# V projected in four 32-column tiles at once, three rounds for four pieces

## The chip, the cores and the metric

The kernel runs on one NeuronCore of a Trainium2 chip. The core has a matrix engine (TensorE, PE in the profile; its weight loads are PEld), a vector engine (VectorE, DVE), a scalar engine (ScalarE, ACT), GpSimd (POOL) and SyncE (SP), which here issues the DMAs that bring weights in. PSUM, where TensorE writes, is handed out in eight tiles by four pools. The metric is device microseconds for one execution.

## What is computed

Four blocks follow each other: A, B, A, B, each added to its input after a layernorm (the same weights both times). A is an attention with a recurrent memory: the 2048 tokens go in 64 segments of 32, and each segment attends over 8 memory rows and its own 32 tokens, with 32 heads of 192. The memory rows of one segment's output are the memory of the next, so segments can't be computed at once. B is a local attention over 8 keys at a distance of 2, with 32 heads of 20.

```python
for s in range(n_seg):
    h = jnp.concatenate([mem, x[:, s*32:(s+1)*32, :]], axis=1)
    q = jnp.einsum('btd,dhe->bhte', h, Wq)
    k = jnp.einsum('btd,dhe->bhte', h, Wk)
    v = jnp.einsum('btd,dhe->bhte', h, Wv)
    scores = jnp.where(mask, jnp.einsum('bhqe,bhke->bhqk', q, k) * scale, -1e9)
    o = jnp.einsum('bhqk,bhke->bhqe', _softmax(scores), v)
    o = jnp.einsum('bhte,hed->btd', o, Wo)
    mem = o[:, :8, :]
    outs.append(o[:, 8:, :])
...
x = x + A(layernorm(x)); x = x + B(layernorm(x))
x = x + A(layernorm(x)); x = x + B(layernorm(x))
```

D is 640 (five chunks of 128 rows, `NCH`), and q, k and v have 6144 columns each.

## The kernel before

**Steps and lanes.** `run` (L517) makes 66 steps and one last. In a step the first A block works on segment s and the second A block on segment s - 2 (`LAG`), side by side as two lanes, so that each weight that is loaded serves 2 x 40 rows: 8 memory rows and 32 tokens for each lane. The rows lie transposed in `ST` (L181), 128 rows of D by chunk, lane and position; there are two such tiles, one for this step and one for the next. Each lane has 64 positions (`SLOT`), of which 40 are used and the rest are zero. The B blocks of the two lanes are done in the same step with the output of the step before.

**Weights.** The four A matrices are cut into 64 halves of 480 KB (`half`, L218): 32 for q and k, 16 for V, 16 for the output. 26 of them stay in SBUF after the first step (`RESIDENT`); the other 38 are read again in every step, from copies in DRAM (`Wr`) that POOL's queue wrote in the first step, into a ring of 7 buffers (`wt`), issued on SP's queue in the order in which they are used. A call of `half` returns a resident tile if there is one; for another half it takes a ring buffer and issues its transfer.

**Order.** The order of TensorE's work is written out by hand in `stages` (L51), and the same in each step; the other engines' instructions are ordered by a scheduler as their inputs come. The names in the plan are:
- q: `qk` (L296), 30 matmuls with 80 moving columns; ACT copies the result to `QK` (L306).
- s: `scores` (L308), 32 small matmuls for a group of four head pieces, then the softmax: three DVE operations, an exp on ACT, three more on DVE, the last of which writes `Pm` (L334).
- t: `p_transpose` (L337), four transposes, and two copies to `PT`, the upper half on DVE and the lower on ACT. PT holds zeros where a lane's queries would meet the other lane's keys.
- v: `v` (L346). The stationary operand is one chunk of `ST` with both lanes, 2 x 64 positions = 128 columns, and the moving one 384 columns of a V half; five matmuls add up a piece in `v_ps`. ACT copies even pieces and DVE odd ones to `vt` (L356, L358). There are 16 pieces, four to a group.
- pv: `pv` (L361), the product of probabilities and V for two pieces, 12 matmuls in two tiles of 64 columns; ACT copies it to `ot`.
- o: `o` (L374), 15 matmuls with `Wo` that add to `acc`; acc holds one of three PSUM tiles of the pool `psA` from the first o to the end of the step; q and v take turns in the others.
- ln1, qkv, logits, e, wo, ln2, store: the B blocks. ln1 and ln2 (`ln_stats`, L271) need a square on POOL (L274) and a sum on DVE (`ssq`, L276) before their last matmul (L280). logits (L444) uses four tiles of 32 columns. e (`b_expand`) has four matmuls and two DVE operations of 0.68 and 1.02 us, five times a step.

At the end of a step `finish_step` writes the memory rows of the next step's `ST` from acc (L395) on DVE; q0 of the next step waits for them.

Of the kernel before, what the change touches and what calls it, by code (L numbers as in the profile page):

```python
# [19 lines left out]
P = 128  # L20
# [9 lines left out]
NP_ = 16  # L30
# [20 lines left out]
def stages():  # L51

    plan = [("q", 0), ("q", 1), ("alpha", 0), ("q", 2), ("q", 3), ("ln1", 0)]
    plan += [("q", 4), ("s", 0), ("v", 0), ("q", 5), ("v", 1), ("qkv", 0), ("q", 6), ("t", 0), ("v", 2), ("q", 7), ("v", 3)]
    for g in (2, 3):
        i, j = 4 * g, 2 * (g - 2)
        extra = [[], [], [("logits", 0)], [("input", 0)], []] if g == 2 else [[("e", c)] for c in range(5)]
        plan += [("q", i), ("s", g - 1)] + extra[0] + [("pv", j), ("v", i - 4)] + extra[1] + [("pv", j + 1), ("q", i + 1)] + extra[2]
        plan += [("o", 2 * j), ("o", 2 * j + 1)] + extra[3] + [("v", i - 3), ("q", i + 2), ("t", g - 1), ("v", i - 2)] + extra[4]
        plan += [("o", 2 * j + 2), ("o", 2 * j + 3), ("q", i + 3), ("v", i - 1)]  # L60
    plan += [("s", 3), ("pv", 4), ("v", 12), ("pv", 5), ("o", 8), ("o", 9), ("v", 13), ("wo", 0), ("v", 14), ("v", 15), ("t", 3)]
    plan += [("o", 10), ("ln2", 0), ("pv", 6), ("pv", 7), ("o", 11), ("store", 0)]
    return plan + [("o", k) for k in range(12, 16)]
# [5 lines left out]
def consumption_order():  # L69

    order = []
    for what, i in PLAN:
        if what == "q":
            order += [2 * i, 2 * i + 1]
        elif what in "vo":
            order.append((32 if what == "v" else 48) + i)
    return order


ORDER = consumption_order()  # L80
RESIDENT = {ORDER[(2 * i + 1) * N_HALVES // (2 * N_RESIDENT)] for i in range(N_RESIDENT)}

# [25 lines left out]
class Kernel:  # L108
    def __init__(self, ctx, tc, A_x, A_mem0, A_Wq, A_Wk, A_Wv, A_Wo, B_wqkv, B_wo, out):
# [16 lines left out]
        self.vp = pool("vp", 6)  # L126
# [6 lines left out]
    def constants(self):  # L133
# [12 lines left out]
        for u in range(2):  # L146
# [3 lines left out]
            nc.gpsimd.memset(m1[SLOT * u:SLOT * u + NM, :], 0.0)  # L150
        self.maskA = cp.tile([P, LT], BF16, name="maskA")
# [34 lines left out]
        self.Pm = [cp.tile([P, 4, 2, SLOT], BF16, name=f"Pm{i}") for i in range(2)]  # L186
# [3 lines left out]
        for t in self.PT:  # L190
            nc.gpsimd.memset(t[:], 0.0)
# [104 lines left out]
    def qk(self, i):  # L296
# [3 lines left out]
        for k in range(2):  # L300
            w = self.half(2 * i + k)[:, :].rearrange("p (c n) -> p c n", c=NCH)
            for m in range(3):
                for c in range(NCH):
                    nc.tensor.matmul(ps[:, 3 * k + m, :, :], lhsT=w[:, c, m * P:(m + 1) * P], rhs=st[:, c, :, 0:LT],  # L304
                                     start=(c == 0), stop=(c == NCH - 1))
# [40 lines left out]
    def v(self, i):  # L346
        nc = self.nc
        w = self.half(32 + i)[:, :].rearrange("p (c n) -> p c n", c=NCH)
        st = self.ST[self.step % 2]
        ps = self.psA.tile([P, UW], F32, name="v_ps", tag="A")  # L350
        for c in range(NCH):
            nc.tensor.matmul(ps[:, :], lhsT=st[:, c, :, :].rearrange("p l t -> p (l t)"), rhs=w[:, c, :],  # L352
# [256 lines left out]
```

## Time and profile before

| what | value |
|---|---|
| median of 3 runs | 3828.19 us (3825.26 to 3828.8) |
| profiled execution, device time | 3827.25 us |
| its span (first to last instruction) | 3825.5 us |
| mean granted TensorE clock | 0.982 |
| read from HBM in all | 1251.42 MB |
| DMA in the first 95 us, by share of 16 engines | 1.04, 353 GB/s |
| end of the first step (first ST from acc, L395) | 149.7 us |
| end of the last full step (last ST from acc) | 3796.5 us |
| mean of the 65 steps between | 56.1 us |
| V matmuls (L352), 128 x 384 | 5280, 330 ns each from start to modelled end, busy 1050 us |
| q and k matmuls (L304) | 31680, busy 1480 us |
| matmuls of logits (L444), four 32-column tiles | 1320, busy 31.9 us |

A matmul's 330 ns is the time from its start to the end of its last row; matmuls overlap, and five V matmuls that stand together occupy TensorE for 0.82 us, as the order of time shows. "Busy" is the time in which at least one was under way. PE's idle time is what other engines, or transfers, or instruction supply ("issue": nothing that the profile shows was waited for) cost it.

### The profile page before, as it was taken

The numbers are of one execution on the slowest core, as the hardware profiler recorded it, in microseconds if no ns is written. First come the engines' busy times: TensorE is split into PE (matmuls) and PEld (weight loads), VectorE is DVE, ScalarE is ACT, GpSimd is POOL, SyncE is SP. The second block draws the span as 40 slices with busy tenths as digits, with TensorE's granted clock in tenths as the row PEclk, the third lists the DMA queues.
The fourth block names the chain that finished last, engine by engine and source line by source line (L and its number), as shares of the span: only waits on it lengthen the run. The fifth ranks groups of instructions, "written<-read, shape, count | busy, mean of one in ns | idle before, by whom it ended". The sixth has DMA issues, their size and how long they took to land.

```text
span 3825.5 us, 172799 instructions
## 1 busy us (share of the span) xinstructions
PE 3515.1 (92%) x79035; PEld 2998.4 (78%) x79035; DVE 2042.5 (53%) x4660; ACT 1501.6 (39%) x3213; POOL 372.0 (10%) x475
## 2 busy tenths in 40 slices
PE   5799999999999999999999999999999999999997
PEld 3578788787888878788787887887788788788886
DVE  1355555545555555555555555555555555555554
ACT  1243443444344344344334434443443444344443
POOL 3110010001001001000100100110010010011000
PEclk7799999999999999999999999999999999999998
DMA  9999999999999999999999999999999999999995
GB/s 353 376 331 341 340 334 344 330 328 337 343 341 337 339 338 338 322 344 341 327 339 340 339 339 342 343 336 331 334 335 338 342 336 346 320 342 342 337 347 211
DMA packets 403276, 1283.94 MB, mean 336 GB/s; under 512 B 41704, under 2 KB 83312, under 8 KB 402544
## 3 DMA queue, kind: packets, MB, share of 16 engines
q1 hardware_dynamic: 397200, 1251.58, 91.4%
q0 software_dynamic: 3040, 18.68, 1.2%
q8 instruction: 617, 10.11, 1.1%
q10 hardware_dynamic: 2304, 2.62, 0.2%
q14 instruction: 115, 0.94, 0.1%
HBM read 1251.42 MB, written 21.30 MB: 333 GB/s over the span
## 4 chain that ended last, share of the span: by engine, by line
PE 74%; DVE 15%; DMA 5%; issue 3%; ACT 1%; SPq 1%; POOLq 0%; POOL 0%; ACTq 0%
PE qk_ps L304 26%; PE v_ps L352 20%; PE acc L385 12%; DVE oT L475 5%; DVE prodv L473 4%; PE qkv_ps L428 4%; PE o_ps L368 3%; PE s_ps L322 3%; PE s_ps L315 3%; DMA x_sb<-in_A_x_dram 2%; DVE vt L358 2%; PE y_ps L482 1%; DMA res<-in_A_Wv_dram 1%; SPq L216 1%; DVE sm L332 1%
## 5 line engine op out<-in xcount | busy, mean ns | idle before, releaser
L306 ACT CAST QK<-qk_ps 128x480 bf16<-128x480 f32 x1056 | 587.3, 556 | 1236.0 <-PE qk_ps L304 1231.6
L304 PE MATMUL qk_ps<-ST,wt 128*128 128x80 bf16 x18810 | 865.5, 203 | 104.6 <-issue 32.6
L304 PEld LDWEIGHTS <-wt 128*128 128x128 bf16 x18810 | 765.3, 100 | 154.3 <-issue 105.7
L352 PEld LDWEIGHTS <-ST 128*128 128x128 bf16 x5280 | 460.9, 99 | 321.9 <-issue 86.3
L304 PE MATMUL qk_ps<-ST,res 128*128 128x80 bf16 x12870 | 614.7, 203 | 32.9 <-issue 16.7
L352 PE MATMUL v_ps<-res,ST 128*128 128x384 bf16 x2970 | 589.0, 330 | 9.5 <-DMA res<-in_A_Wv_dram 6.7
L304 PEld LDWEIGHTS <-res 128*128 128x128 bf16 x12870 | 538.5, 101 | 67.2 <-issue 21.9
L358 DVE CAST vt<-v_ps 128x384 bf16<-128x384 f32 x528 | 292.9, 555 | 520.4 <-PE v_ps L352 512.7
L385 PE MATMUL acc<-ot,wt 128*128 128x80 bf16 x11880 | 530.9, 203 | 9.1 <-DMA wt<-in_A_Wo_dram 4.7
L352 PE MATMUL v_ps<-wt,ST 128*128 128x384 bf16 x2310 | 461.0, 331 | 63.4 <-DVE vt L358 55.0
L385 PEld LDWEIGHTS <-wt 128*128 128x128 bf16 x11880 | 472.4, 100 | 27.7 <-DMA wt<-in_A_Wo_dram 6.9
L356 ACT CAST vt<-v_ps 128x384 bf16<-128x384 f32 x528 | 252.4, 478 | 339.1 <-PE v_ps L352 333.8
L371 ACT CAST ot<-o_ps 128x480 bf16<-128x480 f32 x528 | 292.9, 555 | 224.6 <-PE o_ps L368 216.8
L475 DVE TENSOR_REDUCE oT<-prodv 128x64 bf16<-128x512 bf16 x330 | 335.9, 1018 | 2.2
L435 POOL TENSOR_TENSOR prod<-qT,kh 128x1280 bf16<-128x1280 bf16 x66 | 204.4, 3097 | 735.7 <-ACT kh L430 735.7
L326 DVE TENSOR_TENSOR sb<-s_ps,maskA 128x320 f32<-128x320 f32 x264 | 129.5, 490 | 221.3 <-PE s_ps L322 221.3
L274 POOL TENSOR_TENSOR sq<-x 128x160 f32<-128x160 bf16 x64 | 28.9, 452 | 2162.0 <-DVE x L486 2162.0
L473 DVE TENSOR_TENSOR prodv<-bc_ps,vh 128x512 bf16<-128x512 f32 x330 | 222.9, 676 | 13.3 <-PE bc_ps L470 5.1
L368 PE MATMUL o_ps<-PT,vt 128*64 128x80 bf16 x6336 | 204.0, 206 | 14.3 <-ACT PT L344 13.9
L368 PEld LDWEIGHTS <-vt 128*64 128x64 bf16 x6336 | 153.9, 112 | 75.2 <-issue 55.2
L332 DVE TENSOR_REDUCE sm<-sb 128x8 f32<-128x320 f32 x264 | 128.3, 486 | 123.8 <-ACT sb L330 123.8
L385 PE MATMUL acc<-ot,res 128*128 128x80 bf16 x3960 | 187.2, 203 | 5.5 <-DMA res<-in_A_Wo_dram 5.4
(112 smaller groups left out, 3309.6 us busy)
## 6 DMA issues: line engine op xcount, KB each, us to landing
wt<-Wr SPq DMA_DIRECT2D x2470, 480.0 KB, 5.8
Wr<-wt POOLq DMA_DIRECT2D x38, 480.0 KB, 6.6
wt<-in_A_Wo_dram SPq DMA_DIRECT2D x12, 480.0 KB, 10.8
wt<-in_A_Wq_dram SPq DMA_DIRECT2D x10, 480.0 KB, 11.0
wt<-in_A_Wk_dram SPq DMA_DIRECT2D x9, 480.0 KB, 10.8
res<-in_A_Wv_dram SPq DMA_DIRECT2D x9, 480.0 KB, 11.3
res<-in_A_Wk_dram SPq DMA_DIRECT2D x7, 480.0 KB, 11.2
wt<-in_A_Wv_dram SPq DMA_DIRECT2D x7, 480.0 KB, 11.4
```

The source lines that it names most:

```text
L304: nc.tensor.matmul(ps[:, 3 * k + m, :, :], lhsT=w[:, c, m * P:(m + 1) * P], rhs=st[:, c, :, 0:LT], start=(c == 0), stop=(c == NCH - 1))
L306: nc.scalar.copy(out=self.QK[i % NQK][:, 0:12 * LT], in_=ps[:, :, :, :].rearrange("p m l t -> p (m l t)"))
L332: nc.vector.tensor_reduce(out=sm[:, :], in_=sb[:, :, :], op=ALU.add, axis=AX.X)
L352: nc.tensor.matmul(ps[:, :], lhsT=st[:, c, :, :].rearrange("p l t -> p (l t)"), rhs=w[:, c, :], start=(c == 0), stop=(c == NCH - 1))
L356: nc.scalar.copy(out=vt[:, :], in_=ps[:, :])
L358: nc.vector.tensor_copy(out=vt[:, :], in_=ps[:, :])
L368: nc.tensor.matmul(ps[64 * slot:64 * (slot + 1), jj, n, :, :], lhsT=vt[:, col:col + 64], rhs=self.PT[(i // 4) % 2][:, i % 4, h, :, :], sta ...
L371: nc.scalar.copy(out=ot[:, :, :, :], in_=ps[:, :, :, :, :].rearrange("p j n l t -> p (j n) l t"))
L385: nc.tensor.matmul(self.acc[:, dc, :, :], lhsT=w[:, m % 3, dc * P:(dc + 1) * P], rhs=ot[:, m, :, :], start=(j == 0 and m == 0 and dc == 0) ...
L435: eng.tensor_tensor(out=self.prod[:, :, l, :, :], in0=qT[:, :, l, :].unsqueeze(2).to_broadcast([P, NCH, BW, SEG]), in1=window(kh, l), op=A ...
L473: nc.vector.tensor_tensor(out=pv[:, :, :, :], in0=ps[:, :, :, :], in1=window1(self.vh, c), op=ALU.mult)
L475: nc.vector.tensor_reduce(out=self.oT[:, c, :].rearrange("p (l t) -> p l t", l=2), in_=pv[:, :, :, :].rearrange("p l w t -> p l t w"), op= ...
```

## The change

Three row tiles of 32 tokens stand for the 80 rows: lane 0's tokens, lane 1's tokens, and the 2 x 8 memory rows filled up to 32. They are gathered by POOL in a new tile `SV` once a step (`value_rows`, "rows" in the plan). A V round has four 32-column tiles of TensorE work at once: tiles 0 to 2 multiply the three row tiles by the weights of one piece, and tile 3 multiplies row tile k by the weights of a piece that the three rounds of a group share. So three rounds of 5 x 4 matmuls make four pieces, where four pieces of five matmuls stood. Rows 0 to 95 of the round's result are the piece; rows 96 to 127 are a third of the shared piece, which POOL copies to its rows in a tile `vu`. The list of a round's pieces (`pieces`) has an entry with its half for each of the four tiles. A round's result goes through PSUM and one copy as before, 12 times a step, ACT for even rounds and DVE for odd ones.

Keys are now ordered tokens of both lanes, then memory rows of both lanes. The last step of the softmax writes `Pm` in that order with two multiplications, and both copies after the transpose read 96 rows and multiply by a column of `own`, which is 1 for the keys of one lane and 0 for the other's. pv contracts over 96 rows instead of 128. `ST` loses its padding.

The three rounds of a group stand together in the plan. v11 no longer stands between q15 and s3, and no V piece stands between s0 and qkv, or between wo and ln2. The four shared halves are resident, and the other 22 resident ones are spread over the rest of the order.

```diff
@@ -27,7 +27,7 @@
 SEG = 32
 LT = NM + SEG
 SLOT = 64
-NP_ = 16
+VT = 96
 UW = 384
 HALF = NCH * UW
 NQK = 5
@@ -50,15 +50,14 @@
 
 def stages():
 
-    plan = [("q", 0), ("q", 1), ("alpha", 0), ("q", 2), ("q", 3), ("ln1", 0)]
-    plan += [("q", 4), ("s", 0), ("v", 0), ("q", 5), ("v", 1), ("qkv", 0), ("q", 6), ("t", 0), ("v", 2), ("q", 7), ("v", 3)]
+    plan = [("q", 0), ("rows", 0), ("q", 1), ("alpha", 0), ("q", 2), ("q", 3), ("ln1", 0)]
+    plan += [("q", 4), ("s", 0), ("q", 5), ("qkv", 0), ("q", 6), ("t", 0), ("v", 0), ("v", 1), ("v", 2), ("q", 7)]
     for g in (2, 3):
-        i, j = 4 * g, 2 * (g - 2)
-        extra = [[], [], [("logits", 0)], [("input", 0)], []] if g == 2 else [[("e", c)] for c in range(5)]
-        plan += [("q", i), ("s", g - 1)] + extra[0] + [("pv", j), ("v", i - 4)] + extra[1] + [("pv", j + 1), ("q", i + 1)] + extra[2]
-        plan += [("o", 2 * j), ("o", 2 * j + 1)] + extra[3] + [("v", i - 3), ("q", i + 2), ("t", g - 1), ("v", i - 2)] + extra[4]
-        plan += [("o", 2 * j + 2), ("o", 2 * j + 3), ("q", i + 3), ("v", i - 1)]
-    plan += [("s", 3), ("pv", 4), ("v", 12), ("pv", 5), ("o", 8), ("o", 9), ("v", 13), ("wo", 0), ("v", 14), ("v", 15), ("t", 3)]
+        i, j, r = 4 * g, 2 * (g - 2), 3 * (g - 1)
+        extra = [[], [("logits", 0)], [], [("input", 0)], []] if g == 2 else [[("e", c)] for c in range(5)]
+        plan += [("q", i), ("s", g - 1)] + extra[0] + [("pv", j), ("v", r), ("v", r + 1), ("v", r + 2)] + extra[1] + [("pv", j + 1), ("q", i + 1)] + extra[2]
+        plan += [("o", 2 * j), ("o", 2 * j + 1)] + extra[3] + [("q", i + 2), ("t", g - 1)] + extra[4] + [("o", 2 * j + 2), ("o", 2 * j + 3), ("q", i + 3)]
+    plan += [("s", 3), ("pv", 4), ("v", 9), ("v", 10), ("v", 11), ("pv", 5), ("o", 8), ("o", 9), ("wo", 0), ("t", 3)]
     plan += [("o", 10), ("ln2", 0), ("pv", 6), ("pv", 7), ("o", 11), ("store", 0)]
     return plan + [("o", k) for k in range(12, 16)]
 
@@ -66,19 +65,18 @@
 PLAN = stages()
 
 
...
-RESIDENT = {ORDER[(2 * i + 1) * N_HALVES // (2 * N_RESIDENT)] for i in range(N_RESIDENT)}
+def halves(what, i):
+
+    if what == "q":
+        return [2 * i, 2 * i + 1]
+    if what == "v":
+        return [35 + 4 * (i // 3)] * (i % 3 == 0) + [32 + 4 * (i // 3) + i % 3]
+    return [48 + i] if what == "o" else []
+
+
+SHARED = [35, 39, 43, 47]
+ORDER = [h for what, i in PLAN for h in halves(what, i) if h not in SHARED]
+RESIDENT = set(SHARED) | {ORDER[(2 * i + 1) * len(ORDER) // (2 * (N_RESIDENT - 4))] for i in range(N_RESIDENT - 4)}
 
 
@@ -123,7 +121,8 @@
         self.w1 = pool("w1", 1)
         self.w2 = pool("w2", 2)
         self.w3 = pool("w3", 3)
-        self.vp = pool("vp", 6)
+        self.vp = pool("vp", 5)
+        self.vq = pool("vq", 2)
         self.psA = pool("psA", 3, space=PSUM)
         self.psS = pool("psS", 2, space=PSUM)
         self.psT = pool("psT", 1, space=PSUM)
@@ -148,6 +147,13 @@
             nc.gpsimd.affine_select(out=m1[r, :], in_=m1[r, :], compare_op=ALU.is_ge, fill=NEG, base=0,
                                     pattern=[[-1, LT]], channel_multiplier=1)
             nc.gpsimd.memset(m1[SLOT * u:SLOT * u + NM, :], 0.0)
+        self.own = cp.tile([P, 2], F32, name="own")
+        nc.vector.memset(self.own[:], 0.0)
+        nc.vector.memset(self.own[0:32, 0:1], 1.0)
+        nc.vector.memset(self.own[32:64, 1:2], 1.0)
+        nc.vector.memset(self.own[64:64 + 2 * NM, 1:2], 1.0)
+        nc.vector.memset(self.own[64:64 + NM, 0:1], 1.0)
+        nc.vector.memset(self.own[64:64 + NM, 1:2], 0.0)
         self.maskA = cp.tile([P, LT], BF16, name="maskA")
         nc.vector.tensor_copy(out=self.maskA[:, :], in_=m1[:, :])
 
@@ -177,18 +183,17 @@
         self.wqkv = cp.tile([P, NCH, 3 * D], BF16, name="wqkv")
         self.wo = cp.tile([P, NCH, D], BF16, name="wo")
 
-        self.ST = [cp.tile([P, NCH, 2, SLOT], BF16, name=f"ST{i}") for i in range(2)]
-        for t in self.ST:
+        self.ST = [cp.tile([P, NCH, 2, LT], BF16, name=f"ST{i}") for i in range(2)]
+        self.SV = cp.tile([P, NCH, 3, 32], BF16, name="SV")
+        for t in self.ST + [self.SV]:
             nc.gpsimd.memset(t[:], 0.0)
         self.QK = [cp.tile([P, 12 * LT + SLOT - LT], BF16, name=f"QK{i}") for i in range(NQK)]
         for t in self.QK:
             nc.gpsimd.memset(t[:, 12 * LT:], 0.0)
-        self.Pm = [cp.tile([P, 4, 2, SLOT], BF16, name=f"Pm{i}") for i in range(2)]
+        self.Pm = [cp.tile([P, 4, P], BF16, name=f"Pm{i}") for i in range(2)]
         for t in self.Pm:
             nc.gpsimd.memset(t[:], 0.0)
         self.PT = [cp.tile([P, 4, 2, 2, LT], BF16, name=f"PT{i}") for i in range(2)]
-        for t in self.PT:
-            nc.gpsimd.memset(t[:], 0.0)
         self.zero = cp.tile([P, NCH, SEG], BF16, name="zero")
         nc.gpsimd.memset(self.zero[:], 0.0)
         self.m0T = cp.tile([P, NCH, NM], BF16, name="m0T")
@@ -301,7 +306,7 @@
             w = self.half(2 * i + k)[:, :].rearrange("p (c n) -> p c n", c=NCH)
             for m in range(3):
                 for c in range(NCH):
-                    nc.tensor.matmul(ps[:, 3 * k + m, :, :], lhsT=w[:, c, m * P:(m + 1) * P], rhs=st[:, c, :, 0:LT],
+                    nc.tensor.matmul(ps[:, 3 * k + m, :, :], lhsT=w[:, c, m * P:(m + 1) * P], rhs=st[:, c, :, :],
                                      start=(c == 0), stop=(c == NCH - 1))
         nc.scalar.copy(out=self.QK[i % NQK][:, 0:12 * LT], in_=ps[:, :, :, :].rearrange("p m l t -> p (m l t)"))
 
@@ -331,32 +336,46 @@
         sm = self.w2.tile([P, 8], F32, name="sm")
         nc.vector.tensor_reduce(out=sm[:, :], in_=sb[:, :, :], op=ALU.add, axis=AX.X)
         nc.vector.reciprocal(out=sm[:, :], in_=sm[:, :])
-        nc.vector.tensor_tensor(out=self.Pm[g % 2][:, :, :, 0:LT].rearrange("p a l t -> p (a l) t"), in0=sb[:, :, :],
-                                in1=sm[:, :].unsqueeze(2).to_broadcast([P, 8, LT]), op=ALU.mult)
+        sb4 = sb[:, :, :].rearrange("p (a l) t -> p a l t", l=2)
+        sm4 = sm[:, :].rearrange("p (a l) -> p a l", l=2).unsqueeze(3)
+        for at, n, first in ((0, SEG, NM), (2 * SEG, NM, 0)):
+            nc.vector.tensor_tensor(out=self.Pm[g % 2][:, :, at:at + 2 * n].rearrange("p a (l t) -> p a l t", l=2), in0=sb4[:, :, :, first:first + n],
+                                    in1=sm4.to_broadcast([P, 4, 2, n]), op=ALU.mult)
 
     def p_transpose(self, g):
         nc = self.nc
         ps = self.psT.tile([P, 4, 2, SLOT], BF16, name="pt_ps", tag="T")
         for j in range(4):
             nc.tensor.transpose(out=ps[:, j, :, :].rearrange("p h q -> p (h q)"),
-                                in_=self.Pm[g % 2][:, j, :, :].rearrange("p l t -> p (l t)"), identity=self.ident[:, :])
-        nc.vector.tensor_copy(out=self.PT[g % 2][0:64, :, :, 0, :], in_=ps[0:64, :, :, 0:LT])
-        nc.scalar.copy(out=self.PT[g % 2][64:128, :, :, 1, :], in_=ps[64:128, :, :, 0:LT])
-
-    def v(self, i):
-        nc = self.nc
-        w = self.half(32 + i)[:, :].rearrange("p (c n) -> p c n", c=NCH)
+                                in_=self.Pm[g % 2][:, j, :], identity=self.ident[:, :])
+        pt = self.PT[g % 2]
+        nc.vector.tensor_scalar(out=pt[0:VT, :, :, 0, :], in0=ps[0:VT, :, :, 0:LT], scalar1=self.own[0:VT, 0:1], scalar2=None, op0=ALU.mult)
+        nc.scalar.activation(out=pt[0:VT, :, :, 1, :], in_=ps[0:VT, :, :, 0:LT], func=ACT.Copy, scale=self.own[0:VT, 1:2])
+
+    def value_rows(self):
         st = self.ST[self.step % 2]
+        self.nc.gpsimd.tensor_copy(out=self.SV[:, :, 0:2, :], in_=st[:, :, :, NM:LT])
+        self.nc.gpsimd.tensor_copy(out=self.SV[:, :, 2, 0:2 * NM].rearrange("p c (l t) -> p c l t", l=2), in_=st[:, :, :, 0:NM])
+
+    def v(self, r):
+        nc = self.nc
+        g, k = r // 3, r % 3
+        if k == 0:
+            self.shared = self.half(32 + 4 * g + 3)
+            self.vts[4 * g + 3] = self.vq.tile([VT, UW], BF16, name="vu")
+        pieces = [(t, t, self.half(32 + 4 * g + k)) for t in range(3)] + [(3, k, self.shared)]
         ps = self.psA.tile([P, UW], F32, name="v_ps", tag="A")
         for c in range(NCH):
-            nc.tensor.matmul(ps[:, :], lhsT=st[:, c, :, :].rearrange("p l t -> p (l t)"), rhs=w[:, c, :],
-                             start=(c == 0), stop=(c == NCH - 1))
+            for q, t, w in pieces:
+                nc.tensor.matmul(ps[32 * q:32 * (q + 1), :], lhsT=self.SV[:, c, t, :], rhs=w[:, c * UW:(c + 1) * UW],
+                                 start=(c == 0), stop=(c == NCH - 1), tile_position=(0, 32 * q))
         vt = self.vp.tile([P, UW], BF16, name="vt")
-        if i % 2 == 0:
+        if r % 2 == 0:
             nc.scalar.copy(out=vt[:, :], in_=ps[:, :])
         else:
             nc.vector.tensor_copy(out=vt[:, :], in_=ps[:, :])
-        self.vts[i] = vt
+        nc.gpsimd.tensor_copy(out=self.vts[4 * g + 3][32 * k:32 * (k + 1), :], in_=vt[VT:P, :])
+        self.vts[4 * g + k] = vt
 
     def pv(self, k):
         nc = self.nc
@@ -365,7 +384,7 @@
             i = 2 * k + jj
             vt = self.vts.pop(i)
             for (n, slot, h, col) in ((0, 0, 0, 0), (0, 1, 0, 64), (1, 0, 0, 128), (1, 1, 1, 192), (2, 0, 1, 256), (2, 1, 1, 320)):
-                nc.tensor.matmul(ps[64 * slot:64 * (slot + 1), jj, n, :, :], lhsT=vt[:, col:col + 64], rhs=self.PT[(i // 4) % 2][:, i % 4, h, :, :],
+                nc.tensor.matmul(ps[64 * slot:64 * (slot + 1), jj, n, :, :], lhsT=vt[0:VT, col:col + 64], rhs=self.PT[(i // 4) % 2][0:VT, i % 4, h, :, :],
                                  start=True, stop=True, tile_position=(0, 64 * slot))
         ot = self.w3.tile([P, 6, 2, LT], BF16, name="ot")
         nc.scalar.copy(out=ot[:, :, :, :], in_=ps[:, :, :, :, :].rearrange("p j n l t -> p (j n) l t"))
@@ -543,6 +562,8 @@
                         attend[what](i)
                     elif what in local and b:
                         local[what]()
+                    elif what == "rows" and a:
+                        self.value_rows()
                     elif what == "e" and b:
                         self.b_expand(i)
                     elif what == "alpha" and a and s + 1 < self.n_seg:
```

More of the change, by code (lines that the diff above doesn't have):

```diff
@@ L66 @@
 PLAN = stages()
[L69 to L80, printed above, removed]
-RESIDENT = {ORDER[(2 * i + 1) * N_HALVES // (2 * N_RESIDENT)] for i in range(N_RESIDENT)}
+def halves(what, i):
[7 more added lines that the diff above has]
+RESIDENT = set(SHARED) | {ORDER[(2 * i + 1) * len(ORDER) // (2 * (N_RESIDENT - 4))] for i in range(N_RESIDENT - 4)}
 def window(ap, l):
@@ L341, in p_transpose @@
             nc.tensor.transpose(out=ps[:, j, :, :].rearrange("p h q -> p (h q)"),
[L342 to L349 removed]
+                                in_=self.Pm[g % 2][:, j, :], identity=self.ident[:, :])
[3 more added lines that the diff above has]
+    def value_rows(self):
+        st = self.ST[self.step % 2]
+        self.nc.gpsimd.tensor_copy(out=self.SV[:, :, 0:2, :], in_=st[:, :, :, NM:LT])
+        self.nc.gpsimd.tensor_copy(out=self.SV[:, :, 2, 0:2 * NM].rearrange("p c (l t) -> p c l t", l=2), in_=st[:, :, :, 0:NM])
+    def v(self, r):
+        nc = self.nc
+        g, k = r // 3, r % 3
[3 more added lines that the diff above has]
+        pieces = [(t, t, self.half(32 + 4 * g + k)) for t in range(3)] + [(3, k, self.shared)]
         ps = self.psA.tile([P, UW], F32, name="v_ps", tag="A")
         for c in range(NCH):
[L352 to L353 removed]
+            for q, t, w in pieces:
+                nc.tensor.matmul(ps[32 * q:32 * (q + 1), :], lhsT=self.SV[:, c, t, :], rhs=w[:, c * UW:(c + 1) * UW],
+                                 start=(c == 0), stop=(c == NCH - 1), tile_position=(0, 32 * q))
         vt = self.vp.tile([P, UW], BF16, name="vt")
[L355 removed]
+        if r % 2 == 0:
             nc.scalar.copy(out=vt[:, :], in_=ps[:, :])
```

## The prediction

> **What bounds the kernel now.** I read the page first, then TensorE's waits, then one step in order of time, then windows for the DMA rate. The page's head, DMA issues and chain:
>
> ```profile
> span 3825.5 us, 172799 instructions
> PE 3515.1 (92%) x79035; PEld 2998.4 (78%) x79035; DVE 2042.5 (53%) x4660; ACT 1501.6 (39%) x3213; POOL 372.0 (10%) x475
> ...
> DMA packets 403276, 1283.94 MB, mean 336 GB/s; under 512 B 41704, under 2 KB 83312, under 8 KB 402544
> ...
> PE 74%; DVE 15%; DMA 5%; issue 3%; ACT 1%; SPq 1%; POOLq 0%; POOL 0%; ACTq 0%
> ...
> wt<-Wr SPq DMA_DIRECT2D x2470, 480.0 KB, 5.8
> ```
>
> TensorE (PE) carries the chain. The 2470 streamed transfers are 38 in each of 65 steps, one for each half outside the resident 26. Waits (total us, times, longest):
>
> ```profile
> PE v_ps L352 <- DVE vt L358: 55.4, 66, 1.0
> PE qk_ps L304 <- issue: 49.3, 60, 1.9
> ...
> PE qk_ps L304 <- DMA wt<-Wr: 2.3, 4, 1.0
> ```
>
> PE almost never waits for a streamed half. The SP queue is the one that waits, for PE to give back ring buffers. But little is spare. In the first row below (us, busy of PE, PEld, DVE, ACT, POOL, clock, DMA share, GB/s) is a whole step: DMA share 0.93. The others are the stretches where the DMA has no gap:
>
> ```profile
> 2005.47:2061.00 55.53, 50.28 (x1139) 42.84 (x1139) 32.11 (x74) 22.00 (x47) 5.08 (x6) 1.00 0.93 330
> ...
> 1055.00:1065.00 10.00, 9.73 (x231) 8.39 (x227) 5.65 (x14) 5.63 (x13) 2.89 (x1) 1.00 1.02 398
> 1025.00:1035.00 10.00, 9.02 (x206) 7.68 (x203) 8.71 (x16) 3.74 (x7) 0.00 (x0) 1.00 1.01 393
> 2512.50:2522.00 9.50, 7.82 (x197) 6.83 (x194) 5.42 (x13) 3.81 (x9) 1.03 (x1) 1.00 1.02 406
> ```
>
> About 400 GB/s is what the DMA gives when it is always asked; single windows of 2.5 us reach 419. Keep this number: it decides the case.
>
> **The streamed bytes.** The new v builds its list of pieces with `self.half(32 + 4 * g + k)` inside a comprehension over the three row tiles. `half` remembers resident halves alone; for another it takes a new ring buffer and issues a new 480 KB transfer at each call. So a round whose piece is streamed loads the same half three times, into three of the seven buffers. Which are they? The shared pieces 3, 7, 11, 15 are resident, and every (2i+1) x 60 / 44th of the other 60 in the new order; that makes pieces 1, 6, 8, 13 resident, and pieces 0, 2, 4, 5, 9, 10, 12, 14 streamed: eight, two to a group. Transfers a step: 38 + 2 x 8 = **54**, 54 x 491,520 bytes = 26.54 MB instead of 18.68. With instruction packets, x and output (0.2 MB a step: 1283.94 MB less streams and first load) 26.8 MB. At 400 GB/s: **66.9 us a step**, against today's 56.1 (first memory rows L395 at 149.7 us, last at 3796.5, 65 steps). Bounds: 63.9 by the highest window, 79.7 by today's mean of 336.
>
> For these bytes to hide, PE would have to need as long; it doesn't, as follows.
>
> **The matmuls.** In the order of time:
>
> ```profile
> 2012.06 0.99 PE L352 MATMUL v_ps<-wt,ST 128*128 128x384 bf16 x5
> 2012.88 0.70 PE L304 MATMUL qk_ps<-ST,res 128*128 128x80 bf16 x15
> ...
> 2028.50 0.46 PE L444 MATMUL lg_ps<-prod,E 128*32 128x128 bf16 x20
> 2028.89 0.71 PE L385 MATMUL acc<-ot,res 128*128 128x80 bf16 x15
> ```
>
> A V piece occupies PE for 0.815 us, 163 ns a matmul; sixteen take 13.04 us. The new form, four 32-column tiles with different moving data, is that of L444. Windows of 50 ns on it (matmuls in flight in the first brackets):
>
> ```profile
> 2028.50:2028.55 0.05, 0.05 (x4) 0.05 (x8) 1.00 0.93 384
> 2028.55:2028.60 0.05, 0.05 (x8) 0.05 (x12) 1.00 1.56 461
> 2028.60:2028.65 0.05, 0.05 (x12) 0.05 (x12) 1.00 0.93 384
> ```
>
> Four more start every 50 ns or so, the time of one full 128-column matmul (pt_ps: four in 0.23 us). The tiles stream together. Twelve rounds of 0.815 us are 9.78: -3.26 us. One more edge of tile mode (0.09 us before L444, as much after): +0.1. **-3.15 us of PE work a step.**
>
> **Waits that the new order moves**, on PE:
> - v9's copy on DVE, for which v10 waits today (55.4/66): -0.84.
> - s3 stands right behind q15, without v11 between. q15's copy on ACT ended at 2051.91; s3 would start at 2051.24, and its thirteenth matmul 0.27 later: +0.45.
> - wo is followed by t3, o10, ln2 without v14, v15. y_ps issued its last at 2056.99, ssq was ready at 2058.58 after x, POOL's square and the sum; PE comes to L280 after 0.89: +0.74, less the 0.21 that pv6 waits for PT: +0.53.
> - Odd rounds are copied by DVE while softmax and e fill it (v7 ahead of q13, v9 ahead of v11), each 0 to 1.0: +0.4. t0 and qkv come sooner, 0 to 0.5: +0.15.
> - Instruction supply ("issue", 107 us on all PE rows, 1.65 a step) grows with 160 more matmuls and as many weight loads on some 2390 instructions: by 13% at least, to 3.7 if blocks of short work wait as they do behind s0 today: +0.2 to +2.05.
>
> PE alone would thus need 56.1 - 3.15 + 0.69 + (0.2 to 2.05) = 53.8 to 55.7 us a step. All of that lies beneath 66.9 us of transfers, the gain of 3.15 with it: costed at nothing, and the cover is the DMA. If the cover goes, rival 1 gives the price.
>
> **Other engines.** POOL gets twelve 32x384 copies: its 140- and 160-element copies took 301 and 317 ns, so some 0.5 us (0.30 to 0.92, the latter by its 1280-element multiply of 3097 ns), with value_rows 6.8 us a step where it idles 50. v's copies stand on POOL behind the 3.1 us prod at worst; five vt buffers cover it, else v waits those 3 us. DVE's split multiply adds 0.2 us four times, its scaled PT copies lie between 311 (today's) and 490 ns (float rows), two V casts leave DVE and ACT each; DVE idles 47%. Nothing. On SP, 54 issues at 0.32 to 0.48 us are 22 us of 67: they fit; what stands behind a waiting issue is the next half, in the order of use, and x every fourth step, a step early.
>
> **The first step** ends at 149.7 us and is bound by loading: 362 GB/s over it. The three calls there load 16 halves more and, on POOL's queue, store 16 more to Wr: 15.7 MB, +43 us (0 if PE's waits in it hid it, 47 at the 336 of the mean). Constants and SV are made within it.
>
> **Sum:** 192.7 + 65 x 66.9 + 29 for the last step (3825.5 - 3796.5) = 4570 us of span, +744. The runs' median is 2.7 above the profiled span: **4573 us**.
>
> **Rivals.**
> 1. The other side: the three calls do not cost transfers (asked once, or met from the buffer that is there). Then PE's sum decides: -2.3 to -0.4 a step, **3680 to 3801**. It decides from the point where a step's bytes fit PE's 55 us: up to 44 transfers at 400 GB/s, or 486 GB/s for 54. For it: nothing but that the change speaks of four pieces in three rounds. Against: 2470 transfers today are exactly one a call, and no window reaches 486.
> 2. The ring is too short to keep the DMA full. A V round holds three of seven buffers until it ends, and four in flight at today's 5.8 us to landing are 4 x 0.4915/5.8 = 339 GB/s; with two to three more in the rest of the step, 365: 73.4 us a step, **4997**. PE's clock speaks for it too: in the first 150 us, where PE waits for loads, it was granted 0.75 and 0.66, so a waiting PE gives buffers back later. Against: the windows above held 393 to 406 with the same ring, PE busy.
> 3. A lower ceiling in long stretches: the first 95 us moved 353 GB/s at a DMA share of 1.04. By that 75.9 us a step, **5158**. Against: those loads have shorter rows, and part are stores. The Trainium skill, "DMA: Bandwidth & Descriptors", section Where 436 GB/s comes from, holds that HBM binds HBM-to-SBUF transfers near 358 GB/s for a core; by that a step would take 74.9. The 10 us windows at 393 to 406 differ.
>
> **Numbers.** Forecast (385 to 412 GB/s, 4450 to 4750) 0.66; rival 2 0.20; rival 3 0.09; rival 1 0.05. The range leaves out rivals 1 and 3 and the far part of rival 2: 4420 to 5020. About 0.2%, 8 us, can be told from no change; only rival 1 is near it: faster 0.04, within 0.01, slower 0.95.
>
> **What would show it.** wt from Wr issued 54 x 65 = 3510 times; HBM read near 1.77 GB instead of 1.25; the DMA share 1.0 in nearly all slices at about 400 GB/s; PE busy under 80%, with waits of v_ps and neighbours for DMA wt near 11 us a step as its largest; in windows on V's matmuls four starting every 163 ns. Wrong would be: 2470 issues; a rate below 380; or PE still waiting mostly for engines.

## Result and profile after

| | median, us | ratio to the kernel before, 95% interval |
|---|---|---|
| before, same chip | 3828.49 (3825.26 to 3829.57, 4 runs) | |
| after | 4879.16 (4868.08 to 4888.95, 4 runs) | 1.2745 (1.271 to 1.2781) |

The change makes the kernel 27% slower. The forecast was 4573 us; the measured time is 306 us above it and 118 below rival 2. In what follows a "step" is the mean of the 65 from the first write of memory rows to the last. It takes 71.97 us (180.3 to 4858.3, L414), where it took 56.1.

The page of the changed kernel, the same lines as before:

```profile
span 4887.2 us, 197752 instructions
PE 3859.8 (79%) x89595; PEld 3141.6 (64%) x89595; DVE 2159.5 (44%) x4798; ACT 1491.5 (31%) x3081; POOL 822.3 (17%) x1414
...
DMA packets 564925, 1812.52 MB, mean 371 GB/s; under 512 B 58856, under 2 KB 110704, under 8 KB 564080
...
wt<-Wr SPq DMA_DIRECT2D x3510, 480.0 KB, 6.7
```

3510 streamed transfers are 54 x 65, the number forecast, and the bytes went from 1284 to 1813 MB. PE, busy 92% of the span before, is busy 79%. Its waits (total us, times, longest) say for what:

```profile
PE v_ps L370 <- DMA wt<-Wr: 397.3, 572, 2.3
PE qk_ps L309 <- DMA wt<-Wr: 142.9, 142, 3.3
PE v_ps L370 <- DVE vt L376: 70.4, 56, 1.9
...
PE ln_ps L285 <- DVE ssq L281: 39.6, 65, 1.3
```

With the 8.4 us of acc, PE waits 548.6 us for streamed halves, 8.4 a step; it was 2.3 us in all. The mean rate over the steady part, first in the kernel before, then in the changed one, and four 4-us windows of the latter (columns as in the rows of the prediction):

```profile
150.00:3796.00 3646.00, 3421.38 (x77821) 2928.46 (x77822) 2009.02 (x4583) 1476.99 (x3163) 328.07 (x385) 1.00 0.94 337
```

```profile
180.00:4858.00 4678.00, 3759.84 (x88229) 3068.86 (x88227) 2126.32 (x4715) 1466.63 (x3033) 764.20 (x1294) 0.92 0.98 373
...
2412.00:2416.00 4.00, 2.70 (x72) 2.49 (x69) 1.42 (x4) 0.56 (x1) 0.97 (x2) 1.00 1.01 402
2424.00:2428.00 4.00, 2.31 (x69) 2.21 (x64) 3.93 (x5) 0.95 (x4) 3.19 (x3) 1.00 0.74 293
2428.00:2432.00 4.00, 3.40 (x79) 2.16 (x76) 1.15 (x3) 2.03 (x4) 1.90 (x4) 1.00 0.70 215
2436.00:2440.00 4.00, 3.69 (x65) 2.05 (x60) 2.36 (x6) 1.45 (x3) 0.00 (x0) 0.50 1.02 407
```

The DMA gives 402 and 407 GB/s when it is asked without a break. In the second and third window its share falls to 0.74 and 0.70. By the order of time PE does the B block's qkv there and a resident half of q, waits 1.69 us for nothing shown ("issue"), and then does a V round that gives its three buffers back only at its end: hardly a buffer comes free for some 5 us, and the SP queue has hardly a buffer to fill. A little later PE waits for halves in turn, and its clock stands at 0.50 (last row). The mean is 373 GB/s; a step's 26.8 MB in 71.97 us are 372.

V itself does what the change says. In order of time on PE:

```profile
2399.96 0.34 PE L370 MATMUL v_ps<-wt,SV 128*32 128x384 bf16 x3
2399.97 0.34 PE L370 MATMUL v_ps<-res,SV 128*32 128x384 bf16 x1
2400.13 0.33 PE L370 MATMUL v_ps<-wt,SV 128*32 128x384 bf16 x3
```

Four 32-column matmuls start within 10 ns, and the next four 0.17 us later; in the kernel before, one full matmul started every 163 ns.

### The profile page after: what moved, and what is told of

It is laid out like the page before. It is cut to its first block, busy times and chain, and to the rows that moved or that the text cites. A ratio compares the mean times of both kernels' runs of the same rounds, so it can differ in the third digit from the quotient of the medians.

```text
span 4887.2 us, 197752 instructions
## 1 busy us (share of the span) xinstructions
PE 3859.8 (79%) x89595; PEld 3141.6 (64%) x89595; DVE 2159.5 (44%) x4798; ACT 1491.5 (31%) x3081; POOL 822.3 (17%) x1414
## 3 DMA queue, kind: packets, MB, share of 16 engines
q8 instruction: 700, 11.47, 0.9%
## 4 chain that ended last, share of the span: by engine, by line
DMA 44%; PE 43%; DVE 4%; issue 4%; SPq 2%; ACT 1%; POOL 1%; POOLq 0%; ACTq 0%; DVEq 0%
DMA wt<-Wr 42%; PE qk_ps L309 16%; PE v_ps L370 9%; PE acc L404 8%; PE o_ps L387 2%; PE qkv_ps L447 2%; PE bc_ps L489 1%; DVE Pm L342 1%; SPq L236 1%; DMA Wr<-wt 1%; PE y_ps L501 1%; PE ln_ps L285 1%; PE s_ps L327 1%; PE pt_ps L349 1%; PE s_ps L320 1%
## 5 line engine op out<-in xcount | busy, mean ns | idle before, releaser
L370 PE MATMUL v_ps<-wt,SV 128*32 128x384 bf16 x7920 | 825.0, 375 | 504.3 <-DMA wt<-Wr 397.3
L370 PEld LDWEIGHTS <-SV 128*32 128x32 bf16 x15840 | 507.0, 106 | 1000.6 <-issue 680.3
L309 PE MATMUL qk_ps<-ST,wt 128*128 128x80 bf16 x19800 | 938.6, 205 | 252.1 <-DMA wt<-Wr 142.9
L370 PE MATMUL v_ps<-res,SV 128*32 128x384 bf16 x7920 | 913.8, 381 | 20.8 <-issue 15.7
L377 POOL COPY vu<-vt 32x384 bf16<-32x384 bf16 x792 | 398.7, 503 | 2376.0 <-DVE vt L376 1237.8
L309 PEld LDWEIGHTS <-res 128*128 128x128 bf16 x11880 | 503.3, 103 | 47.4 <-issue 30.5
L376 DVE CAST vt<-v_ps 128x384 bf16<-128x384 f32 x396 | 219.5, 554 | 609.0 <-PE v_ps L370 585.9
L404 PE MATMUL acc<-ot,res 128*128 128x80 bf16 x5940 | 284.9, 204 | 8.5 <-DMA res<-in_A_Wo_dram 5.2
L404 PEld LDWEIGHTS <-res 128*128 128x128 bf16 x5940 | 242.9, 101 | 13.8 <-DMA res<-in_A_Wo_dram 6.3
L342 DVE TENSOR_TENSOR Pm<-sb,sm 128x256 bf16<-128x256 f32 (+1 forms) x528 | 243.0, 501 | 9.3
L447 PE MATMUL qkv_ps<-xnB,wqkv 128*128 128x64 bf16 x4950 | 167.6, 195 | 58.4 <-issue 55.4
```

The source lines that it names most:

```text
L342: nc.vector.tensor_tensor(out=self.Pm[g % 2][:, :, at:at + 2 * n].rearrange("p a (l t) -> p a l t", l=2), in0=sb4[:, :, :, first:first + n ...
L370: nc.tensor.matmul(ps[32 * q:32 * (q + 1), :], lhsT=self.SV[:, c, t, :], rhs=w[:, c * UW:(c + 1) * UW], start=(c == 0), stop=(c == NCH - 1 ...
L376: nc.vector.tensor_copy(out=vt[:, :], in_=ps[:, :])
L377: nc.gpsimd.tensor_copy(out=self.vts[4 * g + 3][32 * k:32 * (k + 1), :], in_=vt[VT:P, :])
L404: nc.tensor.matmul(self.acc[:, dc, :, :], lhsT=w[:, m % 3, dc * P:(dc + 1) * P], rhs=ot[:, m, :, :], start=(j == 0 and m == 0 and dc == 0) ...
L447: nc.tensor.matmul(ps[:, d, :, :], lhsT=self.wqkv[:, c, kind * D + d * P:kind * D + (d + 1) * P], rhs=self.xnB[:, c, :].rearrange("p (l t) ...
```

## Experiments

Kernels are compared with the kernel before on the same chip (3821.61 to 3832.73 us). "Issue" is the sum of all rows of PE's waits that end in "issue".

**1. Ask once.** `own` is requested once a round, 38 transfers a step.

```diff
-        pieces = [(t, t, self.half(32 + 4 * g + k)) for t in range(3)] + [(3, k, self.shared)]
+        own = self.half(32 + 4 * g + k)
+        pieces = [(t, t, own) for t in range(3)] + [(3, k, self.shared)]
```

> The changed kernel with a round's own half asked for once and used by its three row tiles; nothing else differs. Theory (the repeated transfers are the slowdown): 38 streamed transfers a step instead of 54, 2470 in all, HBM read back near 1.25 GB, PE's wait for DMA wt<-Wr under 20 us, and the time is PE's own sum: -3.15 us of matmuls a step, less the waits behind softmax, QK and ssq and the instruction blocks, 3680 to 3830 us, best guess 3775. Rival (tiles, POOL's copies and the new order are the slowdown, the transfers only go along): above 4500 us, since these are unchanged. With it the disputed price of instruction blocks is read: PE's issue rows 110 us if the fetch stays hidden, up to 240 if blocks of short work wait.

Measured: 3952.34 us, ratio 1.0353 (1.0329 to 1.0377), above the theory's range and far below the rival's. Asking once takes back 927 of the 1051 us. But the gain expected from the tiles doesn't come: this kernel is still 131 us slower than the one before, and a step takes 58.1 us. So there is a second cause, which the waits for transfers had covered. PE's waits in this kernel:

```profile
PE qk_ps L309 <- issue: 80.6, 80, 2.5
PE v_ps L371 <- issue: 73.3, 61, 2.7
PE qkv_ps L448 <- issue: 56.3, 38, 2.2
PE s_ps L320 <- ACT QK L311: 39.5, 64, 1.7
PE ln_ps L285 <- DVE ssq L281: 37.5, 63, 1.3
```

Two of the same rows in the kernel before (that of q, 49.3, stands in the prediction):

```profile
PE qkv_ps L428 <- issue: 13.5, 20, 1.3
...
PE v_ps L352 <- issue: 6.2, 9, 1.7
```

Issue is 313.1 us in all, where 240 was expected at most; it was 107.2 before. What "issue" is can be read from where it falls. Here are three stretches, each from the start of work after one such wait to the start after the next one (less 0.04 us, so that the first weight load is within):

```profile
2039.03:2045.25 6.22, 4.82 (x128) 3.54 (x128) 4.39 (x9) 2.44 (x5) 1.33 (x3) 1.00 1.00 395
2045.25:2050.64 5.39, 5.16 (x128) 4.90 (x128) 5.29 (x8) 1.68 (x3) 0.18 (x1) 1.00 0.98 370
2050.64:2056.30 5.66, 4.74 (x128) 3.73 (x128) 4.17 (x9) 2.11 (x4) 0.35 (x2) 1.00 0.97 359
...
q8 instruction: 700, 11.47, 1.1%
```

Each holds 128 matmuls and 128 weight loads, 256 instructions. Over the 600 us from 1000 us on, all 45 stretches between such waits hold 128 weight loads or a whole multiple of it. The page's queue of instructions (last row) carried 700 packets in 11.47 MB, and 2 x 89595 PE instructions are 700 x 256. So PE stops at the ends of its own instruction packets, 5.4 to 6.2 us apart here, until the next one is there; with 294 such waits for 700 packets, it gets past more than half of the ends without one.

**2. Ask once, with waits put right.** ACT copies two of three rounds, q15 and q11 go ahead of an o pair, wo stands behind v11.

```diff
-        plan += [("o", 2 * j), ("o", 2 * j + 1)] + extra[3] + [("q", i + 2), ("t", g - 1)] + extra[4] + [("o", 2 * j + 2), ("o", 2 * j + 3), ("q", i + 3)]
+        plan += [("o", 2 * j), ("o", 2 * j + 1)] + extra[3] + [("q", i + 2), ("t", g - 1)] + extra[4] + [("q", i + 3), ("o", 2 * j + 2), ("o", 2 * j + 3)]
+    plan += [("s", 3), ("pv", 4), ("v", 9), ("v", 10), ("v", 11), ("wo", 0), ("pv", 5), ("o", 8), ("o", 9), ("t", 3)]
...
-        if r % 2 == 0:
+        if k != 1:
```

> As the run before, and three waits of the new order mended: ACT copies the first and third round of every group and DVE only the second; q15 (and q11) stand ahead of the two o of their group, so that o6 and o7 lie between q15 and s3; wo stands right behind v11, with pv5, o8, o9 between it and ln2. If the waits seen in the changed kernel (v_ps for vt on DVE 70 us, ln_ps for ssq 40, s_ps for QK 25) were PE's own time, all three rows fall below 10 us and the kernel gains 100 to 140 us on the run before: 3600 to 3700 us. If PE's instruction supply takes their place, it gains under 50.

Measured: 3948.6 us, 1.0333 (1.0314 to 1.0351). The wait for ssq went and that for QK fell to 24.6 us, but the time fell by 4 us only, as expected for the case that other things take their place: issue rose by 9 us to 322.4, a wait of V's rounds for ACT's copies is new (19.0), and PE's busy time rose by 11.

**3. The old V with three requests.** Only the requests of the change, in the kernel before; copies used in turn, 52 transfers a step.

```diff
-        w = self.half(32 + i)[:, :].rearrange("p (c n) -> p c n", c=NCH)
+        ws = [self.half(32 + i)[:, :].rearrange("p (c n) -> p c n", c=NCH) for t in range(3)]
```

> The kernel before with one edit: v asks for its half three times and its five matmuls use the three copies in turn. No tiles, no new order, no POOL copies. Seven V pieces are streamed in the old order, so 38 + 14 = 52 transfers a step, 25.8 MB with the rest. Theory: bound by the DMA at 372 to 400 GB/s, 64.5 to 69.4 us a step, 4410 to 4730 us in all. Rival (repeated loads hide under PE): 3830 us.

Measured: 4588.32 us, 1.2008 (1.199 to 1.2026), inside the theory's range. The repeated requests alone slow the old kernel as well. The steady part moved 385 GB/s, more than the changed kernel's 373:

```profile
190.00:4550.00 4360.00, 3724.99 (x77672) 3041.45 (x77670) 2016.65 (x4575) 1486.77 (x3157) 327.45 (x384) 0.96 1.01 385
```

**4. Two requests.** The changed kernel, with two requests for a streamed half, 46 transfers a step.

```diff
+        ws = [self.half(32 + 4 * g + k) for t in range(2)]
+        pieces = [(t, t, ws[t // 2]) for t in range(3)] + [(3, k, self.shared)]
```

> The changed kernel with two requests for a streamed half instead of three: 46 transfers a step, 22.9 MB with the rest. If time goes with bytes at 372 to 400 GB/s: 57.2 to 61.5 us a step, 3930 to 4210 us. If only the third copy hurt (a round holding three of seven buffers), it would be at PE's sum, 3700 to 3830.

Measured: 4200.67 us, 1.1002 (1.098 to 1.1024), near the upper end by bytes. Eight transfers from 38 to 46 cost 248 us, and the eight from 46 to 54 cost 678. At 38 the bytes still hide. At 46 the steady part moves 371 GB/s, about the rate of the changed kernel, so the bytes already count; but PE waits 139.1 us for halves in all and 327.0 for issue. Its two largest waits:

```profile
PE v_ps L371 <- DMA wt<-Wr: 101.2, 136, 2.8
PE qk_ps L309 <- issue: 84.8, 95, 2.0
```

**5. Short matmuls in the old V.** Each V matmul of the kernel before in three of 128 columns; nothing else.

```diff
+            for n in range(3):
+                nc.tensor.matmul(ps[:, n * P:(n + 1) * P], lhsT=st[:, c, :, :].rearrange("p l t -> p (l t)"), rhs=w[:, c, n * P:(n + 1) * P],
+                                 start=(c == 0 and n == 0), stop=(c == NCH - 1), skip_group_check=True)
```

> The kernel before, with each V matmul of 384 moving columns split into three of 128, against the same stationary chunk: 240 V matmuls and weight loads a step instead of 80, as many as in the changed kernel, with the same columns streamed, the same tiles, copies, order and transfers. Theory (TensorE's instruction supply is what took the gain of the kernel that asks once: long V matmuls had given the supply time to catch up): the issue rows of PE rise from 107 us to 230-330, and the time to 3930-4060 us. Rival (the supply is no limit, and that kernel lost its gain to the order, to the tiles or to copies on other engines): issue grows by its share of instructions, 13%, and the time is 3830-3870.

Measured: 3987.74 us, 1.0425 (1.0405 to 1.0444), with issue at 244.7: both lie in the range of the theory of instruction supply. Its three largest waits:

```profile
PE qk_ps L304 <- issue: 80.4, 90, 2.3
PE v_ps L353 <- issue: 48.4, 49, 2.2
PE qkv_ps L429 <- issue: 41.8, 33, 2.1
```

The kernel has the old tiles, order and copies, and yet loses 163 us. Issue rises by 137.5 and PE's busy time by 61.0, against which its other waits fall by 37. Five long V matmuls and loads are 10 instructions for 0.82 us of PE; in this form, as in the change's rounds, they are 30 to 40. At 163 ns a pair, PE takes 20.9 us for one packet of V; at 54 ns, or four in 163, it takes 5 to 7.

**6 and 7. No streams.** The kernel before, and the one of experiment 1, with no weight streamed after the first step.

```diff
+        if self.step > 0:
+            return self.resident[min(self.resident, key=lambda r: (abs(r - h), r))]
```

> The kernel before with no weight streamed after the first step: where a streamed half is due, a resident one is multiplied in its place, so the result is another one, with the same instructions on PE, DVE, ACT and POOL. HBM traffic after the first step falls from 336 GB/s to under 10. Theory (instruction packets come late because they share the DMA engines with the weights): the issue rows of PE fall from 107 us to under 30, and the time to 3700-3770. Rival (the supply has a pace of its own, whatever the traffic): issue stays at 80-110 and the time at 3800-3830.

> The changed kernel with each half asked for once a round, and no weight streamed after the first step, as in the run beside it (a resident half is multiplied in its place, so the result is another one). Theory (instruction packets delayed by the weights' traffic ate the gain): the issue rows of PE fall from 313 us to under 70, and the time to 3560-3680, below the quiet form of the kernel before by 60 to 170 us. Rival 1 (the supply has its own pace): issue stays at 250-320 and the time at 3880-3960, above the quiet kernel before. Rival 2 (it is the new waits for copies and sums, not instructions): issue falls, but the time stays above the quiet kernel before.

Measured: 3662.57 us, 0.9574 (0.9558 to 0.959), and 3638.93 us, 0.9513 (0.9499 to 0.9527). In both no row of PE's waits ends in issue any more, so the packets are late only beside the weights' traffic. The streams cost the kernel before 162 us, more than the 55 to 125 expected, and the one that asks once 313. Without them PE's busy time falls as well, by 40 and 92 us; what in the streams makes it longer, no run here shows. PE's busy time, before and once, and then the largest waits of the second:

```profile
PE 3474.9 (95%) x79035; PEld 2982.7 (81%) x79035; DVE 2037.8 (56%) x4660; ACT 1499.2 (41%) x3213; POOL 372.1 (10%) x475
```

```profile
PE 3308.6 (91%) x89595; PEld 2901.6 (80%) x89595; DVE 2225.2 (61%) x4798; ACT 1452.2 (40%) x3081; POOL 785.8 (22%) x1398
```

```profile
PE pt_ps L351 <- DVE Pm L344: 92.5, 65, 1.4
PE s_ps L322 <- ACT QK L313: 61.9, 68, 1.1
PE ln_ps L287 <- DVE ssq L283: 39.5, 65, 1.3
PE qkv_ps L450 <- ACT qT L452: 32.1, 65, 0.6
```

PE's work fell by 166.3 us, 2.56 a step. The four waits are new, 226.0 us; gone are v10's wait for v9's copy (64.1) and pv's for PT (14.0). That leaves -18, and the spans differ by 23.6. This lies between the theory (issue gone, and faster) and rival 2 (no faster): the rest of the expected 60 to 170 us went into waits for the softmax, for q's copy, for the sum and for qT even with an idle DMA.

**8. Wider tile.** The tokens of both lanes in one tile of 64 columns beside two of 32: 180 V matmuls a step.

```diff
+            for at, n, rows_, w in ((0, 64, self.SV[:, c, 0:2, :], own), (64, 32, self.SV[:, c, 2, :], own), (96, 32, self.SV[:, c, k, :], self.shared)):
+                lhsT = rows_.rearrange("p l t -> p (l t)") if n == 64 else rows_
+                nc.tensor.matmul(ps[at:at + n, :], lhsT=lhsT, rhs=w[:, c * UW:(c + 1) * UW],
+                                 start=(c == 0), stop=(c == NCH - 1), tile_position=(0, at))
```

> The changed kernel with each half asked for once a round, and the tokens of both lanes as one tile of 64 columns beside two of 32: 180 V matmuls and loads a step instead of 240. If tiles of different widths stream together (163 ns for three): the issue rows of PE fall from 313 us to 200-260 by the theory of instruction supply and the time from 3952 to 3840-3900; without that theory it stays at 3940-3960. If tiles of different widths wait for each other: a round of V takes 1.2 to 1.6 us instead of 0.82, and the time is 4200-4600.

Measured: 5121.16 us, 1.3375 (1.3338 to 1.3413), beyond even the slower expectation. In order of time:

```profile
2407.59 0.60 PE L371 MATMUL v_ps<-wt,SV 128*64 128x384 bf16 x2
2407.85 0.34 PE L371 MATMUL v_ps<-res,SV 128*32 128x384 bf16 x1
2408.12 0.62 PE L371 MATMUL v_ps<-wt,SV 128*64 128x384 bf16 x2
```

Three matmuls take 0.53 to 0.55 us where four equal tiles took 0.163, and a round takes 2.7 us. The two 32-column tiles start together. But from the 64-column tile to them, and from them to the next, it is 0.26 to 0.28 us each time: tiles of different widths did not stream together, and each change cost some 0.1 us more than a start every 163 ns. The Trainium skill, "TensorEngine Tiling (Array Packing)", section Key Properties, says that a change of tiling mode drains TensorE; the trace agrees, with 0.26 to 0.28 us between starts. Beside this slow V, issue falls to 109.9 us with 669 packets, which fits the theory that long work lets the supply catch up.

**9. A deeper ring.** The changed kernel with `RING` 11 and `N_RESIDENT` 22, 58 transfers a step.

> The changed kernel with eleven ring buffers instead of seven, paid for with four resident halves: 58 transfers a step instead of 54, 28.8 MB. If the 372 GB/s of the changed kernel comes from too short a ring (lulls with all buffers full or held): 395 to 410 GB/s, 70 to 73 us a step, 4760 to 4950 us. If 372 is the DMA's own ceiling in this pattern: 77 us a step, 5200 to 5250 us.

Measured: 4788.25 us, 1.2501 (1.2473 to 1.253). It moves 7% more bytes in 2% less time:

```profile
183.00:4754.00 4571.00, 3717.32 (x88217) 3027.39 (x88217) 2130.31 (x4714) 1452.14 (x3033) 756.89 (x1294) 0.95 1.02 409
```

409 GB/s for 4.6 ms, 70.3 us a step. This is the first case of the expectation: 373 came from the short ring, and is no ceiling of the DMA.

**10 to 12. Fewer transfers in flight.** Experiment 2 and the kernel before with `RING` 5 and `N_RESIDENT` 28, and then experiment 2 with seven buffers and at most four transfers in flight:

```diff
+            if len(self.streamed) >= 4:
+                self.nc.sync.dma_start(out=self.marks[len(self.streamed) % 8][:, :], in_=self.streamed[-4][0:1, 0:32])
             self.nc.sync.dma_start(out=t[:, :], in_=self.Wr[h][:, :])
+            self.streamed.append(t)
```

> The form that asks once, with the changed order, with five ring buffers and 28 resident halves instead of seven and 26: 36 transfers a step instead of 38. Theory A (an instruction packet waits behind all the weights in flight, so fewer in flight let it through sooner): issue rows of PE fall from 322 us to 180-250, and the time from 3949 to 3830-3900. Theory B (the packet's delay depends on how busy the DMA engines are, not on the depth of the weights' queue): issue 280-310 by the 5% less traffic, time 3910-3950. Against both: the short ring makes PE wait for weights, over 50 us of DMA waits, and the time stays or grows.

> The kernel before with five ring buffers and 28 resident halves, 36 transfers a step. Theory A: issue rows of PE fall from 107 us to 50-80 and the time to 3760-3800. Theory B: issue 90-105, time 3800-3830. Against both: DMA waits of over 50 us and a time of 3850 or more.

> The form that asks once, with the changed order, seven ring buffers and 26 resident halves as before, but at most four streamed transfers in flight: ahead of each one, SP's queue issues a 64-byte copy out of the half issued four earlier, which waits until that has landed. Theory A (the packets of instructions wait behind the weights in flight): the issue rows of PE fall from 322 us to 80-160, while the two or three buffers more than in the run with five keep PE's waits for weights under 100 us (246 there); time 3780-3860, under or at the kernel before. Rival (what fell with five buffers fell because PE waited for weights instead, which gave the supply time): issue falls only as far as DMA waits grow, their sum stays at 290-340 us, and the time is 3930-4020.

Measured: 4014.95 us, 1.049 (1.046 to 1.052); 3883.16 us, 1.0132 (1.0108 to 1.0155); 3929.34 us, 1.028 (1.0257 to 1.0303). Beside the others (us of the profiled runs):

| | issue | PE's waits for streamed halves | sum | span |
|---|---|---|---|---|
| before | 107 | 2 | 109 | 3825.5 |
| before, 5 buffers | 10 | 122 | 132 | 3882.9 |
| once | 313 | 7 | 320 | 3945.6 |
| once, order mended | 322 | 13 | 335 | 3945.2 |
| the same, 5 buffers | 79 | 246 | 325 | 4012.2 |
| the same, 4 in flight | 291 | 57 | 348 | 3939.3 |
| two requests (experiment 4) | 327 | 139 | 466 | 4196.4 |

With five buffers issue falls far below what either theory expected, waits for halves take its place, and the time grows, which is the outcome that both expectations name as against the two theories:

```profile
PE qk_ps L309 <- DMA wt<-Wr: 164.2, 215, 2.6
PE acc L405 <- DMA wt<-Wr: 81.4, 73, 3.1
```

Had the packets come sooner because fewer weights were in flight, the run with four in flight would have kept that fall without those waits. It did not; its sum, 348, misses the rival's band of 290 to 340 by a little. The reading that fits the first six rows is the rival's: while PE waits for halves, the next packet arrives. But this is argued and not shown. The cap is a weak test: 38 transfers a step of 58.1 us at 6.0 us to landing are some 3.9 in flight on the mean in experiment 2 (an estimate; 3.3 with five buffers), so a cap of four takes off only the peaks. And experiment 4, with 5.0 by the same estimate, fits neither theory well: its packets are hardly later than with 3.9, and its 139 us of waits for halves take nothing off issue, though its heavier traffic, 371 GB/s against 326, makes it no clean comparison. Why a packet is late beside the streams, by turns on the DMA engines or by the memory, was not settled. No kernel with the streams left in beat the one before.

## Why the prediction came out as it did

**The cause and the sign were right.** Three requests make three transfers: 3510 of them, HBM read 1770 MB (forecast "near 1.77 GB"), PE busy 79% (under 80). Experiment 1 shows it by undoing it, experiment 3 by doing it alone. PE's waits for halves, forecast near 11 us a step, are 8.4.

**The rate was mis-sized.** "At 400 GB/s: 66.9 us a step" took windows of 10 us, in which the DMA was always asked, as the mean of whole steps. The changed kernel has stretches in which it isn't: 372 GB/s and 71.97 us. The term is 65 x 5.07 = +330 us. The first step cost +30.6 instead of +43 (-12), and the last 28.9 as forecast: together the +317 between the sum and the span. By its own test ("a rate below 380") this step of the forecast was wrong, and its mechanism is that of rival 2, the ring too short, at a milder price (372, not 365). That 4879 lies within 4420 to 5020 is owed to the part of rival 2 that this range takes in; the forecast's own 4450 to 4750 does not hold it. Experiment 9 tells it from rival 3: 409 GB/s held for the whole run. The Trainium skill, "DMA: Bandwidth & Descriptors", section Where 436 GB/s comes from, puts the limit from HBM near 358 GB/s; this measurement stands above it and decides.

**PE alone, "53.8 to 55.7 us a step", was wrong,** though hidden beneath the transfers. Experiment 1 takes 58.1, and so rival 1's 3680 to 3801 became 3952. Two steps of that sum failed. The larger miss is "-3.15 us of PE work": beside the streams PE's busy time falls from 3515.1 to 3400.8 us only, 1.76 a step, 1.4 short. The other is "+0.2 to +2.05" for instruction supply: it grew by 206 us, 3.2 a step, 1.1 above the bound. The bound was scaled from packets as they ran before, and missed that the long V matmuls were the very time in which the supply caught up; experiment 5 shows that with the old tiles. The Trainium skill, "Runtime: NRT & Kernel Launch", section Instruction fetch mechanics, has packets of 256 instructions and calls the crossing mostly hidden. The size agrees; the rest doesn't: with the streams the waits at the crossings cost 107 to 322 us here in kernels that seldom wait for weights, and only without the streams nothing.

**The smaller terms.** PE's work, -1.76 beside the streams, is -2.56 in the quiet pair; the four tiles stream in 163 to 170 ns as read from L444. ssq's wait is 0.58 to 0.61 a step (0.74 forecast), s3's 0.38 in the changed kernel (0.45 forecast), and POOL's row copy 503 ns (0.5). Copies of odd rounds were put at 0.4 and cost 70.4/65 = 1.08 (v11 waits up to 1.9 us for v9's copy), in the changed kernel alone: experiment 1 has no such row. The wait of t for Pm, up to 1.42 a step in the quiet kernel, was not in the sum; "t0 and qkv come sooner, 0 to 0.5" was too small for it and for qT's 0.49.

## What to carry to other kernels

Count the calls of a helper that issues a transfer; inside a comprehension one expression can be three of them, and with the DMA near its rate each one is time. A steady rate is read over whole steps, with the stretches in which nobody frees a buffer, and not over the best windows. Before long matmuls are cut into short ones that stream the same columns, count the instructions per us and look where the waits without a releaser fall: if they lie 256 PE instructions apart, the long ones were paying for the supply.

## What was unexpected in the hardware

- Weights' traffic slows other transfers and the supply of instructions: without it the kernel before loses all 107 us of issue and 162 us in all, and a 160 KB store on ACT's queue lands 1.8 us after its issue instead of 5.7.
- Waits for instructions and for halves traded places at 36 and 38 transfers a step (issue from 79 to 322 us, sums of 320 to 348), but not at 46, where issue stayed at 327 beside 139 us for halves.
- Column tiles of 64 and 32 did not stream together: each change of width took 0.26 to 0.28 us from start to start, while four tiles of 32 follow four others after 0.163.
- Where PE had waited for halves, its granted clock stood at 0.50 in windows of 4 us, and at 0.92 over the steady part against 1.00 before.
